# Sliding attention in two pieces instead of three, gate matmuls moved, and the first two row tiles of x transposed on TensorE

## The chip, the core and the metric

The kernel runs on one core of one Trainium2 chip. The metric is the device time of one execution in microseconds (us). A core has five engines that run side by side, each through its own in-order list of instructions: TensorE (PE in the profile; its weight loads are PEld), VectorE (DVE), ScalarE (ACT), GpSimd (POOL) and SyncE (SP), which here only issues DMA transfers.

## The reference

Two attention blocks on the same x (2048 rows, 1024 columns, bf16) are mixed by a gate. Each has 32 heads of width 32.

```python
x = A_x
g = _sigmoid((x * gate_w).sum(-1, keepdims=True))
a = _A_ref(x, A_wqkv, A_wo)      # linear attention
b = _B_ref(x, B_wqkv, B_wo)      # sliding, dilated attention
return g * a + (1 - g) * b

# A: q, k, v = split of x @ wqkv; phi(t) = where(t > 0, t + 1, exp(t)) + 1e-6
#    kv = sum_s phi(k) v;  z = sum_s phi(k);  o = (phi(q) kv) / (phi(q) z + 1e-6);  a = o @ wo
# B: row s sees the W = 8 rows s, s-2, ..., s-14 (dil = 2; rows below 0 are masked)
#    attn = softmax(q k * Dh**-0.5) over them;  o = attn v;  b = o @ wo
```

## The kernel before

**Parity.** A row of B sees only rows of its own parity, so all work is split into two halves p of 1024 rows (even and odd rows). In a half the window is 8 neighbouring rows. A half has 8 row tiles of 128 rows; row tile t of the kernel is tile t % 8 of half t // 8. x is held transposed in `xT[p]`; `xt_load` (L88) brings one row tile by a transposing DMA on SP.

**Products.** Most matrix products are done as seven block products of half-sized blocks in place of eight (a Strassen scheme). A `Group` (L238) is one such product: m1, m2, m3, m6, m4, m7, m5, each four matmuls of 512 columns (named a product here; out groups have eight). Sums of blocks of x (`xsums`, into SS) and of weights (`Weights.sums`, into T, TS) are made on VectorE ahead of use. Two PSUM banks, X and Y, serve a group: m1 writes X, ScalarE copies it to M1s; m6 adds onto X, ScalarE copies it to U2s; m5 adds onto X, copied to U4s; m3 adds onto X and ScalarE writes the result out. m2, m7 and m4 use Y, and VectorE adds M1s, U4s or U2s to it. `run` (L413) interleaves a group g with the one before it, p, in the order m1(g), m2(g), m3(p), m6(g), m4(p), m7(g), m5(g). Groups: vb (V of B), k and q (of B, for 8 heads and one half), ka and va (K and V of A), qa, and out.

**Side work.** After each product `side` lets a step of a queue in: generators yield (delay, length), and a step is taken when its delay is over and the last one's length has passed. In this way the pieces of B's attention (`attn`, L659), of A's key-value sums (`kv`, L543) and of A's outputs (`qa_out`, L580) are put between products. TensorE and SP follow the program's order as written; for the other engines a scheduler orders the instructions when the kernel is built.

**The sliding attention.** For each of 8 (nn, p), 8 heads as two chunks of four (ch): `scores(t)` multiplies blocks of 57 queries with the 64 keys that they can see, four heads side by side (48 matmuls, L672), ScalarE takes the exponential into PT (L678), VectorE multiplies with the mask `maskp` (L680). `pv(t)` multiplies PT with V (48 matmuls, L690) and with ones for the denominators (8 matmuls over 342 columns, L696); ScalarE forms the reciprocal as exp(-ln) in rB (L702, L704), VectorE copies the numerator to nB (L703) and multiplies into oB (L706), which SP stores in OB_d (L707). A piece t covers a third of the rows of both chunks: 18 blocks of 57 are 1026 rows, so that V_d and OB_d have 1026 rows and kT and qT two columns more than needed. One PSUM tile of four banks (tag "s") serves every side piece in turn: scores, pv, kv and qa_out.

**phi.** When a ka group's row is done, `phi` (L518) takes an exponential of 1024 columns on ScalarE (eA) and three VectorE steps.

**Gates.** `gate(t)` (L438) is 8 matmuls of one column on row tile t of xT, into the PSUM tile gps. Tiles 0 to 7 of half 0 are pairs 0 to 3 (tile c and c + 4), those of half 1 pairs 4 to 7. `gates(4)` stands after `vb_group(2)`, `gates(5)` after `vb_group(3)`.

**Start.** `warm_up` (L451) issues matmuls on zeros. `vb_load(k, j)` brings a quarter of one half of V's weights: (0, 0) on ScalarE's queue, all others on SP. `vb_plain(0, 1)` (L484) computes four row tiles with plain products (the tile K, L495), with groups of three warm-ups between; only then do the Groups begin.

**End.** Plain products of A's queries (`qa_plain`, the tile Q), two qa groups, and eight out groups. The oA pieces feed POOL (obA), SP stores them in OA_d, and `out_load` (L757) reads OB_d and, by transposing DMA, OA_d into oT for the out groups.

Of the kernel before, what the change touches and what calls it, by code (L numbers as in the profile page):

```python
# [8 lines left out]
ACT = mybir.ActivationFunctionType  # L9
# [8 lines left out]
TW = 6 * QB  # L18
SPAN = 3 * TW
# [8 lines left out]
def kernel(  # L28
# [30 lines left out]
    V_d = [dram.tile([SPAN, D], BF16, name=f"V_d{p}") for p in range(2)]  # L59
    OB_d = [dram.tile([8, P, SPAN], BF16, name=f"OB_d{p}") for p in range(2)]  # L60
# [115 lines left out]
    bview = B_wqkv.rearrange("(k p) n -> p k n", p=P)  # L176
    gw = consts.tile([P, 8], BF16, name="gw")
    nc.gpsimd.dma_start(out=gw[:], in_=gate_w.rearrange("(k p) -> p k", p=P))

    def vb_load(k, j):  # L180
        (nc.scalar if (k, j) == (0, 0) else nc.sync).dma_start(out=W[:, 2 * k:2 * k + 2, 512 * j:512 * j + 512],
                          in_=bview[:, 2 * k:2 * k + 2, 2 * D + 512 * j:2 * D + 512 * j + 512])
    vb_load(0, 0)
    xt_load(0)
    for k in range(1, 4):
        vb_load(k, 0)
    for t in (4, 1, 5):
        xt_load(t)
# [13 lines left out]
    maskp = consts.tile([P, 2, 6, QB], BF16, name="maskp")  # L202
    nc.gpsimd.memset(maskp[:, :, 0, :], 0.0)
    for w in range(8):
        for base in (7 - w, 71 - w):
            nc.gpsimd.affine_select(out=maskp[:, 0, 0, :], in_=maskp[:, 0, 0, :], compare_op=ALU.not_equal,
                                    fill=1.0, base=base, pattern=[[1, QB]], channel_multiplier=-1)
        nc.gpsimd.affine_select(out=maskp[0:64, 1, 0, :], in_=maskp[0:64, 1, 0, :], compare_op=ALU.not_equal,
                                fill=1.0, base=-w, pattern=[[1, QB]], channel_multiplier=-1)
    nc.gpsimd.tensor_copy(out=maskp[64:P, 1, 0, :], in_=maskp[64:P, 0, 0, :])  # L210
    for e in range(1, 6):
        nc.gpsimd.tensor_copy(out=maskp[:, 0, e, :], in_=maskp[:, 0, 0, :])
        nc.gpsimd.tensor_copy(out=maskp[:, 1, e, :], in_=maskp[:, 1 if e == 3 else 0, 0, :])
    ones = consts.tile([P, 32], BF16, name="ones")
    nc.gpsimd.memset(ones[:], 1.0)
    for p in range(2):
        nc.gpsimd.dma_start(out=V_d[p][1024:SPAN, :].rearrange("r (a e) -> (r a) e", e=P), in_=warm[0:16, 0:P])
# [128 lines left out]
    def step(force=False):  # L346
        seen = set()
        for entry in list(queue):
            if entry[4] in seen:
                continue  # L350
            seen.add(entry[4])
            if not force and (entry[0] > state["now"] or state["free"] > state["now"]):
                continue
            state["free"] = state["now"] + entry[3]
            try:
                delay, entry[3] = next(entry[1])
                entry[0] = state["now"] + delay
                state["steps"] += 1
                return True
            except StopIteration:  # L360
                queue.remove(entry)
                return step(force)
        return False
# [90 lines left out]


# [28 lines left out]
    def vb_plain(*pairs):  # L484


        vs = {pair: v_tiles("va") for pair in pairs}
        tiles = [(pair, i) for pair in pairs for i in range(2)]

        def ps_of(pair, i):  # L490
            return ps_pj.tile([P, 512], F32, name="K", tag="XY"[i] + str(pair % 2))

        def mm(ps, pair, i, j, kc):
            p, c = divmod(pair, 4)
            nc.tensor.matmul(ps[:], lhsT=xT[p][:, kc, i, c * P:c * P + P],  # L495
                             rhs=wvB.W[:, kc, 512 * j:512 * j + 512], start=kc == 0, stop=kc == 7,
                             skip_group_check=True)
        for pair, i in tiles:
            ps = ps_of(pair, i)
            for kc in range(8):  # L500
                if (pair, i) == tiles[0] and kc in (2, 4, 6):
                    warm_up(3)
                mm(ps, pair, i, 0, kc)
            gate(tile_of(pair, i))
            v_final(vs[pair], True)(i, 0, ps[:], None)
        tiles = tiles[2:] + tiles[:2]
        ps = {t: ps_of(*t) for t in tiles}
        for k in range(4):
            for t in tiles:
                for kc in (2 * k, 2 * k + 1):  # L510
                    mm(ps[t], *t, 1, kc)
                if k == 3:
                    pair, i = t
                    v_final(vs[pair], True)(i, 1, ps[t][:], None)
                    vb_store(vs[pair], pair, i)
# [24 lines left out]
    def va_group(w, pair):  # L540
        vs = v_tiles("vA")

        def kv():  # L543
# [18 lines left out]
            if last:  # L562
                nc.vector.tensor_tensor(out=KVz[:].rearrange("p c (g e) -> p c g e", g=4),
                                        in0=KVacc[:, :, None, :].broadcast_to([P, 8, 4, 33]),
                                        in1=bd[:, None, :, :].broadcast_to([P, 8, 4, 33]), op=ALU.mult)
            yield 2, 2
# [89 lines left out]
    def q_of(t, j, b):  # L656
        return TW * t + 2 * QB * j + QB * b

    def attn(nn, p, kT, qT, vw):  # L659

        def scores(t):
            s = side_ps("s")
            for ch in range(2):
                for j in range(3):
                    e = (3 * ch + j) * QB
                    for b in range(2):
                        q0 = q_of(t, j, b)
                        k0 = max(0, q0 - 7)  # L670
                        for g in range(4):
                            nc.tensor.matmul(s[64 * b:64 * b + 64, g, e:e + QB],  # L672
                                             lhsT=kT[32 * g:32 * g + 32, 1024 * ch + k0:1024 * ch + k0 + 64],
                                             rhs=qT[32 * g:32 * g + 32, 1024 * ch + q0:1024 * ch + q0 + QB],
                                             start=True, stop=True)
            PT = ptp.tile([P, 4, TW], BF16, name="PT", tag="PT")
            with tc.high_priority():
                nc.scalar.activation(out=PT[:], in_=s[:, :, 0:TW], func=ACT.Exp, scale=SCALE)  # L678
            m = maskp[:, 0 if t else 1, :, :].rearrange("p i q -> p (i q)")
            nc.vector.tensor_tensor(out=PT[:], in0=PT[:], in1=m[:, None, :].broadcast_to([P, 4, TW]), op=ALU.mult)  # L680
            return PT

        def pv(t, PT):
            o = side_ps("o")
            for e in range(6):
                ch, j = divmod(e, 3)
                for g in range(4):
                    for b in range(2):
                        rows = slice(64 * b, 64 * b + 64)
                        nc.tensor.matmul(o[32 * g:32 * g + 32, 2 * b, QB * e:QB * e + QB],  # L690
                                         lhsT=vw[rows, 3 * t + j, 4 * ch + g, :],
                                         rhs=PT[rows, g, QB * e:QB * e + QB], start=True, stop=True)
            for g in range(4):
                for b in range(2):
                    rows = slice(64 * b, 64 * b + 64)
                    nc.tensor.matmul(o[32 * g:32 * g + 32, 2 * b + 1, 0:TW], lhsT=ones[rows, :], rhs=PT[rows, g, :],  # L696
                                     start=True, stop=True)
            nB = ofp.tile([P, 2, TW], F32, name="nB", tag="nB", bufs=1)
            rB = ofp.tile([P, 2, TW], F32, name="rB", tag="rB", bufs=1)
            oB = ofp.tile([P, 6, 2, QB], BF16, name="oB", tag="oB", bufs=2)  # L700
            with tc.high_priority():
                nc.scalar.activation(out=rB[:], in_=o[:, 1:4:2, 0:TW], func=ACT.Ln)  # L702
                nc.vector.tensor_copy(out=nB[:], in_=o[:, 0:4:2, 0:TW])  # L703
            nc.scalar.activation(out=rB[:], in_=rB[:], func=ACT.Exp, scale=-1.0)  # L704
            num, r = (ap.rearrange("p b (e q) -> p e b q", e=6) for ap in (nB[:], rB[:]))
            nc.vector.tensor_tensor(out=oB[:], in0=num, in1=r, op=ALU.mult)  # L706
            nc.sync.dma_start(out=OB_d[p][2 * nn:2 * nn + 2, :, TW * t:TW * t + TW].rearrange("c p q -> p c q"),  # L707
                              in_=oB[:].rearrange("p (c j) b q -> p c (j b q)", c=2))

        last = None  # L710
        yield 0, 2
        for t in range(4):
            if t < 3:
                PT = scores(t)
                yield (1, 3) if last else (3, 3)
            if last:
                pv(*last)
                yield 1, 3
            last = (t, PT)

    def load_v(nn, p):
        vw = vwp.tile([P, NPAIR, 8, 32], BF16, name="vw", tag="vw")
        for b, j, n in ((0, 0, 1), (0, 1, 8), (1, 0, 9)):
            k0 = max(0, q_of(0, j, b) - 7)
# [7 lines left out]
    def k_group(w, nn, p):  # L732
        kT = kqp.tile([P, 2050], BF16, name="kT", tag="kq")
        nc.gpsimd.memset(kT[:, 2048:2050], 0.0)
        its[nn, p] = kT
        return Group(col_ops(w, p), lambda i, j, ps, add: acc(kT[:, 1024 * j + 512 * i:1024 * j + 512 * i + 512], ps, add))

    def q_group(w, nn, p):
        qT = kqp.tile([P, 2050], BF16, name="qT", tag="kq")
        nc.gpsimd.memset(qT[:, 2048:2050], 0.0)  # L740
# [5 lines left out]
        return Group(col_ops(w, p), lambda i, j, ps, add: acc(qT[:, 1024 * j + 512 * i:1024 * j + 512 * i + 512], ps, add), done)  # L746
# [89 lines left out]
    warm_up(24)  # L836
# [27 lines left out]
    for f in (ws[0], ws[1], xs[0], xs[1], ws[2], xs[3], ws[3], xs[2]):  # L864
        f()
# [4 lines left out]
    gates(4)  # L870
# [4 lines left out]
    gates(5)  # L875
# [104 lines left out]
```

## Time and profile before

| what | value |
|---|---|
| median of 3 runs | 463.4 us (463.18 to 464.05) |
| the profiled execution | 462.85 us, of which 461.1 us are the span |
| TensorE busy | 450.9 us (98%), 5137 matmuls |
| VectorE, ScalarE, GpSimd busy | 286.1, 241.6, 56.6 us |
| moved by DMA | 51.65 MB |

The span runs from the first to the last instruction. In a timeline line stand the start and the length of a run of like instructions, the engine (PE, DVE, ACT), the line of the kernel, operation, written tile <- read tiles, shapes and count; in brackets the idle time before it and what ended it. Lengths of matmuls overlap, since they are pipelined, so what a matmul costs is seen from start to start. In a line of the waits stand who waited for whom, then the total in us, the number of times, and the longest.

### The profile page before, as it was taken

Reading aid. Unit: us, or ns where it says so; the run is one execution under the profiler, and the core shown is the slowest. Engines: PE = TensorE matmul, PEld = TensorE weight load, DVE = VectorE, ACT = ScalarE, POOL = GpSimd, SP = SyncE. Lnnn points to the kernel's source line nnn. Section 1 sums busy time; section 2 is a strip of 40 time slices with the busy share of each in tenths; the row PEclk is TensorE's granted clock in tenths of the full one; section 3 lists DMA queues with packets and bytes.
Section 4 is the critical chain, followed back from the end, with each engine's and each line's share of the span. In section 5 each row is a group of like instructions: output and inputs, shape, how many; then the busy total and the mean of one; then the engine's idle time right before and its main releaser. Section 6 shows DMA issues by size and latency. Waiting matters only on the chain. (4 is left out here: it accounts for less than half of the span.)

```text
span 461.1 us, 11964 instructions
## 1 busy us (share of the span) xinstructions
PE 450.9 (98%) x5137; PEld 217.7 (47%) x5137; DVE 286.1 (62%) x458; ACT 241.6 (52%) x367; POOL 56.6 (12%) x130
## 2 busy tenths in 40 slices
PE   8989999999999999999999999999999999999997
PEld 5445444444444444444444444445554444444444
DVE  0547668769848577486684856579876973164312
ACT  1233447568568386584855848536676545222221
POOL 8000000000000000000000000006676313000000
PEclk9999999999999999999999999999999999999999
DMA  8999811590211702106021066464239872699211
GB/s 180 187 221 246 275 41 64 147 256 19 57 28 33 157 21 64 22 20 159 18 71 28 17 146 181 112 188 103 68 77 205 177 171 81 118 189 174 68 47 46
DMA packets 117941, 51.65 MB, mean 112 GB/s; under 512 B 77696, under 2 KB 115840, under 8 KB 117888
## 3 DMA queue, kind: packets, MB, share of 16 engines
q1 hardware_dynamic: 117520, 50.62, 47.1%
q8 instruction: 40, 0.66, 0.6%
q10 hardware_dynamic: 272, 0.26, 0.2%
q0 software_dynamic: 96, 0.01, 0.1%
q14 instruction: 13, 0.11, 0.1%
HBM read 25.69 MB, written 16.79 MB: 92 GB/s over the span
## 5 line engine op out<-in xcount | busy, mean ns | idle before, releaser
L252 PEld LDWEIGHTS <-xT 128*128 128x128 bf16 (+1 forms) x352 | 32.6, 98 | 37.6 <-issue 0.6
L252 PE MATMUL X<-T,SS 128*128 128x512 f16 x176 | 45.2, 379 | 0.0
L635 PE MATMUL Q<-xT,WS 128*128 128x512 bf16 x192 | 43.9, 379 | 0.5 <-DVE vA L234 0.5
L261 ACT COPY U4s<-X 128x512 f32<-128x512 f32 x40 | 23.2, 581 | 37.3 <-PE X L252 37.2
L252 PEld LDWEIGHTS <-WS 128*128 128x128 bf16 (+1 forms) x288 | 27.1, 98 | 32.9 <-issue 2.5
L678 ACT ACTIVATE PT<-s 128x1368 bf16<-128x1368 f32 x24 | 31.5, 1314 | 19.9 <-PE s L672 19.9
L252 PE MATMUL Y<-W,xT 128*128 128x512 bf16 (+1 forms) x152 | 39.1, 380 | 0.0
L252 PEld LDWEIGHTS <-SS 128*128 128x128 f16 x264 | 24.4, 98 | 27.8
L252 PE MATMUL Y<-xT,WS 128*128 128x512 bf16 (+1 forms) x144 | 37.0, 379 | 0.2 <-DVE qT L234 0.2
L252 PE MATMUL X<-SS,TS 128*128 128x512 f16 x144 | 36.9, 379 | 0.1
L680 DVE TENSOR_TENSOR PT<-PT,maskp 128x1368 bf16<-128x1368 bf16 x24 | 20.8, 867 | 20.8 <-ACT PT L678 20.8
L252 PEld LDWEIGHTS <-TS 128*128 128x128 f16 x216 | 20.5, 98 | 25.2 <-issue 1.8
L261 ACT COPY M1s<-X 128x512 f32<-128x512 f32 x40 | 23.3, 583 | 11.8 <-PE X L252 11.7
L261 ACT COPY U2s<-X 128x512 f32<-128x512 f32 x40 | 23.3, 582 | 10.4 <-PE X L252 10.4
L635 PEld LDWEIGHTS <-WS 128*128 128x128 bf16 x192 | 18.2, 98 | 20.6 <-issue 0.8
L252 PEld LDWEIGHTS <-oT 128*128 128x128 bf16 (+1 forms) x176 | 17.1, 98 | 21.8 <-DMA oT<-OA_d 1.5
L703 DVE COPY nB<-o 128x684 f32<-128x684 f32 x24 | 20.8, 867 | 6.3 <-ACT rB L702 6.0
L603 POOL TENSOR_TENSOR obA<-ofv,rec 128x512 bf16<-128x512 f32 x22 | 24.0, 1109 | 0.9
L640 ACT ACTIVATE eq<-Q 128x512 bf16<-128x512 f32 x24 | 14.3, 598 | 18.4 <-PE Q L635 17.3
L252 PE MATMUL X<-T,oS 128*128 128x512 f16 x96 | 22.7, 379 | 0.0
L252 PE MATMUL X<-W,SS 128*128 128x512 bf16 x88 | 22.7, 380 | 0.0
L252 PE MATMUL X<-W,xT 128*128 128x512 bf16 x88 | 22.6, 380 | 0.0
(137 smaller groups left out, 759.6 us busy)
## 6 DMA issues: line engine op xcount, KB each, us to landing
OB_d<-oB SPq DMA_DIRECT2D x24, 171.0 KB, 2.9
V_d<-va SPq DMA_DIRECT2D x16, 256.0 KB, 3.0
WS<-in_B_wqkv_dram SPq DMA_DIRECT2D x16, 256.0 KB, 4.2
W<-in_A_wqkv_dram SPq DMA_DIRECT2D x8, 512.0 KB, 7.0
OA_d<-obA SPq DMA_DIRECT2D x16, 256.0 KB, 2.4
out_dram<-osb SPq DMA_DIRECT2D x30, 128.0 KB, 2.0
oT<-OB_d SPq DMA_DIRECT2D x12, 256.0 KB, 4.8
vw<-V_d SPq DMA_DIRECT2D x8, 288.0 KB, 4.7
```

The source lines that it names most:

```text
L252: nc.tensor.matmul(ps[:], lhsT=lhsT, rhs=rhs, start=start and kc == 0, stop=kc == self.nk - 1, skip_group_check=True)
L261: nc.scalar.copy(out=s[:], in_=ps[:])
L603: nc.gpsimd.tensor_tensor(out=ob[:, k:k + 2], in0=of[:, k:k + 2, :, 0:32], in1=rec[:, k:k + 2].broadcast_to([P, 2, 8, 32]), op=ALU.mult)
L635: nc.tensor.matmul(ps[:], lhsT=w.W[:, kc, j * P:j * P + P], rhs=xT[p][:, kc, i, :], start=kc == 0, stop=kc == 7, skip_group_check=True)
L640: nc.scalar.activation(out=es[i][:, j, :], in_=ps[:], func=ACT.Exp)
L678: nc.scalar.activation(out=PT[:], in_=s[:, :, 0:TW], func=ACT.Exp, scale=SCALE)
L680: nc.vector.tensor_tensor(out=PT[:], in0=PT[:], in1=m[:, None, :].broadcast_to([P, 4, TW]), op=ALU.mult)
L703: nc.vector.tensor_copy(out=nB[:], in_=o[:, 0:4:2, 0:TW])
```

## The change

- **Pieces**: `scores` and `pv` take one chunk of four heads over all 1024 rows (9 pairs of blocks, the last of 56 instead of 57): 72 matmuls a piece in place of 48, the exponential and the mask over 4 x 512 columns, the ones over 512. There are two pieces of each kind instead of three. Their order is scores, scores, pv, pv instead of scores, scores, pv, scores, pv, pv, with other delays between. oB has one buffer instead of two. One mask serves all pieces, and V_d, OB_d, kT and qT have exactly 1024 rows or columns; the fills for the rows beyond are gone. `load_v` issues four DMAs instead of three.
- **Gates**: `gates(4)` moves behind `vb_group(3)`.
- **Start**: row tiles 0 and 4 are loaded as they are (`xr`), and TensorE transposes them (8 transposes each, with an identity made on POOL) into PSUM, from where ScalarE and VectorE copy one half each into xT. 14 warm-ups stand ahead instead of 24, and none between. The first sums on VectorE are issued after the last of these copies.
- **Guard**: oA pieces are not taken before KVz is computed.

```diff
+    ident = consts.tile([P, P], BF16, name="ident")
+    nc.gpsimd.memset(ident[:], 0.0)
+    nc.gpsimd.affine_select(out=ident[:], in_=ident[:], compare_op=ALU.not_equal, fill=1.0, base=0,
+                            pattern=[[1, P]], channel_multiplier=-1)
...
-    vb_load(0, 0)
-    xt_load(0)
-    for k in range(1, 4):
-        vb_load(k, 0)
-    for t in (4, 1, 5):
+    xr = {}
+
+    def xr_load(t):
+        xr[t] = ering.tile([P, D], BF16, name="xr", tag="e")
+        nc.sync.dma_start(out=xr[t][:], in_=xrows(t))
+    vb_load(0, 0, nc.scalar)
+    xr_load(0)
+    vb_load(1, 0)
+    vb_load(2, 0)
+    vb_load(3, 0)
+    xr_load(4)
+    for t in (1, 5):
         xt_load(t)
...
-    maskp = consts.tile([P, 2, 6, QB], BF16, name="maskp")
-    nc.gpsimd.memset(maskp[:, :, 0, :], 0.0)
+    maskp = consts.tile([P, 512], BF16, name="maskp")
+    nc.gpsimd.memset(maskp[:], 0.0)
...
     for w in range(8):
...
+        diagonal(slice(0, QB), -w)
+        diagonal(slice(QB, 2 * QB), 7 - w)
+        diagonal(slice(QB, 2 * QB), 71 - w)
+        diagonal(slice(8 * QB, 512), 72 - w)
...
-    for p in range(2):
-        nc.gpsimd.dma_start(out=V_d[p][1024:SPAN, :].rearrange("r (a e) -> (r a) e", e=P), in_=warm[0:16, 0:P])
...
+            if entry[4] == "oa" and "KVz" not in ready:
+                continue
...
+    def transpose(t):
+        p, j = divmod(t, 8)
+        hf, c = divmod(j, 4)
+        for k0, tag, copy in ((0, "X1", nc.scalar.copy), (4, "Y1", nc.vector.tensor_copy)):
+            tps = ps_pj.tile([P, 512], F32, name="tps", tag=tag)
+            tps = tps.bitcast(BF16)[:, 0:512].rearrange("p (k n) -> p k n", k=4)
+            for k in range(4):
+                nc.tensor.transpose(tps[:, k, :], xr[t][:, (k0 + k) * P:(k0 + k + 1) * P], ident[:])
+            with tc.high_priority():
+                last_dve[0] = copy(out=xT[p][:, k0:k0 + 4, hf, c * P:(c + 1) * P], in_=tps).ins
...
             for kc in range(8):
-                if (pair, i) == tiles[0] and kc in (2, 4, 6):
-                    warm_up(3)
+                if (pair, i) == tiles[0] and kc in (0, 6):
+                    transpose(tile_of(pair, kc // 6))
                 mm(ps, pair, i, 0, kc)
...
+    def block(j, b):
+
+        q0 = 2 * QB * j + (QB if j < 8 else QB - 1) * b
+        return q0, QB if j < 8 else QB - 1, min(max(0, q0 - 7), 960)
...
+        def scores(ch):
             s = side_ps("s")
...
+            for j in range(NPAIR):
+                for b in range(2):
+                    q0, n, k0 = block(j, b)
+                    for g in range(4):
+                        nc.tensor.matmul(s[64 * b:64 * b + 64, g, QB * j:QB * j + n],
+                                         lhsT=kT[32 * g:32 * g + 32, ch, k0:k0 + 64],
+                                         rhs=qT[32 * g:32 * g + 32, ch, q0:q0 + n], start=True, stop=True)
+            PT = ptp.tile([P, 4, 512], BF16, name="PT", tag="PT")
             with tc.high_priority():
-                nc.scalar.activation(out=PT[:], in_=s[:, :, 0:TW], func=ACT.Exp, scale=SCALE)
...
+                nc.scalar.activation(out=PT[:], in_=s[:], func=ACT.Exp, scale=SCALE)
+            nc.vector.tensor_tensor(out=PT[:], in0=PT[:], in1=maskp[:, None, :].broadcast_to([P, 4, 512]), op=ALU.mult)
             return PT
...
+                    nc.tensor.matmul(o[32 * g:32 * g + 32, 2 * b + 1, :], lhsT=ones[rows, :], rhs=PT[rows, g, :],
                                      start=True, stop=True)
...
+            oB = ofp.tile([P, 1024], BF16, name="oB", tag="oB", bufs=1)
             with tc.high_priority():
...
+                nc.scalar.activation(out=rB[:], in_=o[:, 1:4:2, :], func=ACT.Ln)
+                nc.vector.tensor_copy(out=nB[:], in_=o[:, 0:4:2, :])
             nc.scalar.activation(out=rB[:], in_=rB[:], func=ACT.Exp, scale=-1.0)
...
+            nc.sync.dma_start(out=OB_d[p][2 * nn + ch, :, :], in_=oB[:])
...
-        last = None
-        yield 0, 2
-        for t in range(4):
-            if t < 3:
-                PT = scores(t)
-                yield (1, 3) if last else (3, 3)
-            if last:
-                pv(*last)
-                yield 1, 3
-            last = (t, PT)
+        yield 0, 4
+        PT = [scores(0)]
+        yield 1, 4
+        PT.append(scores(1))
+        for ch in range(2):
+            yield 1, 3
+            pv(ch, PT[ch])
+        yield 1, 3
...
-        for b, j, n in ((0, 0, 1), (0, 1, 8), (1, 0, 9)):
+        for b, j, n in ((0, 0, 1), (0, 1, 8), (1, 0, 8), (1, 8, 1)):
...
-        kT = kqp.tile([P, 2050], BF16, name="kT", tag="kq")
-        nc.gpsimd.memset(kT[:, 2048:2050], 0.0)
+        kT = kqp.tile([P, 2, 1024], BF16, name="kT", tag="kq")
...
-    warm_up(24)
+    warm_up(14)
...
+    with tc.issue_after(last_dve[0]):
+        for f in (ws[0], ws[1], xs[0], xs[1], ws[2], xs[3], ws[3], xs[2]):
+            f()
     later(2, lambda: gates(3))
...
     run(lambda: vb_group(2), 0)
     x_loads(6, 7)
-    gates(4)
     defer(1, xsums(4) + xsums(1))
     run(lambda: vb_group(3), 0)
...
-    gates(5)
+    gates(4, 5)
```

## The prediction

> **What bounds the kernel now.** I read the page's first part, the waits of TensorE, and then the timeline of each stage that the change touches.
>
> ```profile
> span 461.1 us, 11964 instructions
> ...
> PE 450.9 (98%) x5137; PEld 217.7 (47%) x5137; DVE 286.1 (62%) x458; ACT 241.6 (52%) x367; POOL 56.6 (12%) x130
> ```
> ```profile
> PE gps L442 <- DMA xT<-in_A_x_dram: 1.5, 2, 1.1
> ...
> PE X L252 <- DMA oT<-OA_d: 1.0, 1, 1.0
> ...
> PE s L672 <- DVE nB L703: 0.6, 1, 0.6
> PE Q L635 <- DVE vA L234: 0.5, 1, 0.5
> ```
>
> TensorE is busy 98% of the span, so time moves only by work that leaves TensorE's in-order stream, or by waits that leave it or enter it. The start (TensorE timeline):
>
> ```profile
> 1.20 4.52 PE L453 MATMUL gps<-KVacc 128*128 128x256 bf16 x24 [1.20 <-DVE KVacc L171]
> 5.56 0.59 PE L495 MATMUL K<-W,xT 128*128 128x512 bf16 x2
> ...
> 7.39 0.59 PE L495 MATMUL K<-W,xT 128*128 128x512 bf16 x2 [0.91 <-DMA W<-in_B_wqkv_dram]
> ...
> 9.04 0.59 PE L495 MATMUL K<-W,xT 128*128 128x512 bf16 x2
> ```
>
> The first tile of K moves at the pace of W: its last three blocks land at 7.35, 8.03 and 9.00 us. From 9.04 the stream is dense. Then the gates:
>
> ```profile
> 27.00 1.03 PE L252 MATMUL X<-T,SS 128*128 128x512 f16 x4
> 28.45 0.35 PE L442 MATMUL gps<-gw,xT 128*128 128x1 bf16 x8 [0.43 <-DMA xT<-in_A_x_dram]
> 29.91 0.35 PE L442 MATMUL gps<-gw,xT 128*128 128x1 bf16 x8 [1.11 <-DMA xT<-in_A_x_dram]
> 30.12 1.02 PE L252 MATMUL X<-W,xT 128*128 128x512 bf16 x4
> ```
>
> TensorE stands before row tiles that have not landed. Last, one attention on TensorE, and ScalarE beside it:
>
> ```profile
> 134.60 0.57 PE L672 MATMUL s<-qT,kT 32*64 32x57 bf16 x48
> 135.11 1.04 PE L252 MATMUL X<-W,SS 128*128 128x512 bf16 x4
> ...
> 138.16 0.37 PE L696 MATMUL o<-PT,ones 64*32 64x342 bf16 x8
> 138.46 1.04 PE L252 MATMUL Y<-xT,WS 128*128 128x512 f16 x4
> ...
> 140.20 1.03 PE L252 MATMUL X<-W,xT 128*128 128x512 bf16 x4
> 141.27 0.56 PE L672 MATMUL s<-qT,kT 32*64 32x57 bf16 x48
> ```
> ```profile
> 135.24 1.31 ACT L678 ACTIVATE PT<-s 128x1368 bf16<-128x1368 f32 x1 [0.81 <-PE s L672]
> 136.45 0.58 ACT L232 CAST tA<-X 128x512 bf16<-128x512 f32 x1
> 137.06 1.06 ACT L520 ACTIVATE eA<-tA 128x1024 bf16<-128x1024 bf16 x1
> 138.03 0.57 ACT L261 COPY U2s<-X 128x512 f32<-128x512 f32 x1
> ```
>
> A product (4 matmuls) takes 0.864 us from start to start. m5 starts two products after m6's end and adds onto the bank that U2s copies; m3, two products after m5's, onto the one that U4s copies. A copy that is late stops TensorE. The ScalarE queue is in order.
>
> **The change part by part** (profiled execution: 462.85 us with a span of 461.1; median of the runs 463.4, so 0.55 more).
>
> *Pieces.* From start to start, a scores piece of 48 matmuls adds 0.595 us to TensorE, a PV piece of 48+8 0.755. In the single records 32 matmuls go at once (0.14 us), then after a break of 0.10 one each 8.35 ns; a piece also pays about 0.09 to enter and, in scores, 0.13 to leave. With 72 matmuls: scores 0.595 + 24 x 0.00835 = 0.795. PV: 0.755 + 0.200 + the longer tail of the ones, 170 columns more at 0.42 ns = 0.071 (all eight run side by side, or the tail would be longer than 0.25): 1.026. Each of 8 attentions: before 3 x (0.595 + 0.755) = 4.05, after 2 x (0.795 + 1.026) = 3.64. Saved 0.41 x 8 = 3.3 us.
>
> *Waits that go with the old order.* Scores 3 waits for nB at 3 products after PV 1: 0.12 us in six attentions (141.27 above: due at 141.16), 0.63 in the first; and the 0.5 before Q at 302 (0.65 from start to start), behind the last PV piece, which now lies four products ahead. Gone: 0.7 + 0.6 + 0.65 = 2.0.
>
> *The new wait.* The pieces are now scores, 4 products, scores, 4, PV, 3, PV. The second scores comes right after m3 of a ka group, and ScalarE's order becomes: tA cast, first phi exponential (eA), PT, U2s; before, PT went ahead of both. Counted from m3's start in the seven attentions that have a ka group: cast at 0.864 + 0.20 = 1.06; eA 0.61 later, 1.67; ScalarE is free 0.96 on, 2.63. The scores are over by 0.864 + 0.795 = 1.66, so PT waits for eA. PT's length: 1.314 us for 1368 columns, 0.735 for 684, hence 0.84 ns a column and 1.88 for 2048; the next starts 0.1 before its end, so U2s runs 4.41 to 4.99. m5 is due at 1.66 + 2.59 = 4.25 and starts at 5.05: **0.80 us of wait, 7 times, 5.6 us.** Behind it on TensorE everything stands; on ScalarE the second eA and U4s go later, which the PV piece doesn't need. In the scores before (after m7) U4s ends at 2.49 with m3 due at 2.59: hidden, by 0.05 to 0.1 only.
> PV 2 needs nB: Ln over 1024 is 1.02 (0.735 + 340 x 0.84 ns), nB after it 1.22 (0.867 for 684 columns, 0.686 for 512, so 1.05 ns a column), and 2.6 are there; the mask over 2048 (1.2), kT and eA stand ahead of nB on VectorE, which makes it about even (0.05 each), and 0.65 late in the second attention, where two of wvA's 1.22 us sums lie between. Cost 0.95. With one oB, the second oB waits on VectorE for the OB_d store (2.9 us to land): about 1 us, with va's add queued behind it; that add has a product to spare, so nothing.
>
> *Gates.* From 27.86, where the last product ends, to 30.12 are 2.26 us, of which 16 gate matmuls take 0.40 where nothing is late. Moved one group (6 us) later they meet landed tiles (the next pair lands at 31.1 and 32.7): saved 1.86. Their number stays. Group 3 itself needs only pair 3, whose gates ran without a wait at 24.87, and its last VectorE sum is at 29.7, with its m7 due at 32.2.
>
> *Start.* Removed: 10 warm-ups ahead and 9 between. Added: 16 transposes, four copies, and the identity on POOL (its gw issue, 1.08 us, lies between; ready near 3). On SP a plain load issues in 0.46 us against 1.3, and lands in 0.8 us steps (W: 14.18, 14.97, 15.68) against 1.4 for transposing ones. So vb1 to vb3 land near 5, 6 and 6.5, xr 4 near 7.3. TensorE: 14 warm-ups at 0.213 end at 4.2; 8 transposes and a copy (0.58 plus 0.2 of delay) put the first K at 5.4; two thirds of a tile, then the wait for xr 4; transposes, rest, gates: the second tile at about 8.8 against 9.84. Gain 1.0, between -0.3 and 1.7. Behind the new copies stand, on ScalarE, the va casts (the first is due only after a whole tile), and on VectorE wvB's sums, which wait for W's second half anyway (15.06 before, near 12 now). In VectorE's new order the sum of row tile 6 stands ahead of the second W sum; even if that tile lands at 19.95 as before, this W sum is over at 21.5 and the x sum after it at 21.9, with m6 due at 24.3. The other four sums need 3.1 us more, to 25.0, with m7 due at 25.1: just hidden, and with earlier x tiles by 2 us.
> The transposes' price: the nearest row is the gate, 8 loads of 128x128 weights with a short matmul in 0.20 to 0.37 us; a warm-up of 256 columns takes 0.109. I take 0.06 to 0.11 each. The Trainium skill (TensorE: Matmul & The Clock Gate, Part 4: PE-mode transpose) speaks against it: about 275 ns each in a kernel, and transposes do not count as busy for the clock. At 275 ns, 16 take 4.4 us and the start loses about 0.8. The row decides: a warm-up too lasts 0.42 us by its record, at 0.21 from start to start. On the clock the trace says that warm-ups run 0.213 apart up to 4.6 us and 0.109 from 4.9; the same page (Part 1) asks for about 3.4 us of activity. Fourteen last only 3.0. If the half clock stays until 8, six K matmuls take 0.43 instead of 0.216, partly under the wait for W: the gain falls to 0.2.
>
> *The rest.* Fewer waits for credits put the eighth oA piece four Q matmuls (0.86 us) earlier against out(0), whose wait for oT hangs on it over POOL, the OA_d store and SP (13.3 us from piece to landing, TensorE's work 12.5): saved 0.86. Nothing: 8 more vw issues against 8 fewer OB_d on SP, hidden since SP waits 161 us for oB; two V_d fills and 16 small memsets off POOL, and a mask of 32 selects instead of 24, done near 12 us and first used at 103; the oa guard. Without that cover the mask would cost 0.18 us a select.
>
> Sum: -3.3 - 2.0 + 5.6 + 0.95 - 1.86 - 1.0 - 0.86 = -2.5, thus 460.4 in the profiled execution and **460.9 us** as a median.
>
> **Rivals.**
> *The ScalarE stall is not there* (0.10): if eA comes after PT on the chip as before, 5.6 and the nB cost go: 455. For it: ScalarE is idle 48%. Against: its program order is fixed.
> *The start gives nothing* (0.14): cold clock, or xr 4 after 8 us: 462 to 462.6. For it: fourteen warm-ups are short. Against: transposes and K follow at once.
> *PT costs more than its columns* (0.18, slower): four full banks in one exponential. Each 0.1 us on top adds 0.7 to the seven waits, and past the 0.05 of slack it also delays U4s and so m3, in all eight attentions, and in the first attention's m5. The sign turns at 2.07 instead of 1.88 us (7 x 0.19 + 9 x 0.14 = 2.5); at 2.15 it is 7 x 0.27 + 9 x 0.22 = 3.9 us: 464.8. For it: slack of 0.05 is all there is. Against: 684 and 1368 columns, and 1056 in a copy at 1.036, lie on one line.
>
> **How the numbers follow.** The forecast has 0.58, 459.3 to 462.3. What a measurement can tell is 0.2%, 0.9 us: faster is below 462.5. Faster: 0.56 of the forecast, 0.10, and 0.04 of the start rival: 0.70; the same: 0.02 + 0.10: 0.12; slower 0.18. The range leaves out the first rival and half of the last: 458.6 to 463.8.
>
> **What would show it.** Right: PT 128x2048 at 1.88 us with eA just before it in seven attentions, TensorE waiting for ACT U2s about 0.8 each; no gps wait near 28; scores at 0.8 and PV at 1.03 from start to start; K's second tile near 8.8. Wrong: no such wait for U2s, a wait of m3 for U4s, or K matmuls 0.43 apart.

## The result, and the profile after

| | before | after |
|---|---|---|
| median | 463.29 us (4 runs, 462.98 to 464.05) | 460.69 us (4 runs, 460.46 to 461.02) |
| ratio of the times | | 0.9942, interval 0.9925 to 0.9959 |
| the profiled execution | 462.85 us | 460.67 us |

The changed kernel is 2.6 us faster by the medians, 2.2 by the two profiled executions. In the experiments below, ten of the 25 executions of the kernel before have a mean granted clock of 0.995 or 0.996 and a median 1.7 us above that of the other 15, which have 0.999 or 1.0; "at full clock" means there an execution at 0.998 or more. The first part of its page, and all waits of TensorE:

```profile
span 458.9 us, 11765 instructions
...
PE 446.0 (97%) x5070; PEld 216.0 (47%) x5070; DVE 282.9 (62%) x452; ACT 237.1 (52%) x345; POOL 60.8 (13%) x119
```
```profile
PE X L264 <- ACT U2s L273: 4.5, 7, 0.7
PE tps L476 <- DMA xr<-in_A_x_dram: 1.2, 1, 1.2
PE gps L467 <- DVE KVacc L170: 1.2, 1, 1.2
PE K L520 <- DMA W<-in_B_wqkv_dram: 0.7, 1, 0.7
PE o L712 <- DVE nB L724: 0.6, 1, 0.6
PE K L520 <- ACT xT L478: 0.5, 1, 0.5
PE o L712 <- issue: 0.3, 1, 0.3
```

Of the four waits that were shown of before (gates for xT, X for oT, scores for nB, Q for vA) none is left. In their place stand seven waits for U2s, one PV that waits for nB, and, at the start, one for the second row tile of x. These rows count idle time between the modelled ends of matmuls; from start to start the seven U2s waits are 0.77, 0.77, 0.83, 0.83, 0.83, 0.83 and 0.83 us, together 5.69, against 4.5 in the row.

One attention on TensorE, and ScalarE beside it, at the same place as before (the m5 that waits starts at 137.21):

```profile
133.14 0.77 PE L696 MATMUL s<-qT,kT 32*64 32x57 bf16 x72
133.84 1.04 PE L264 MATMUL X<-SS,TS 128*128 128x512 f16 x4
...
135.57 1.03 PE L264 MATMUL Y<-xT,WS 128*128 128x512 f16 x4
137.21 1.02 PE L264 MATMUL X<-SS,TS 128*128 128x512 f16 x4 [0.61 <-ACT U2s L273]
138.16 0.74 PE L712 MATMUL o<-PT,vw 64*32 64x57 bf16 x72
```
```profile
133.24 0.59 ACT L244 CAST tA<-X 128x512 bf16<-128x512 f32 x1 [0.68 <-PE X L264]
133.86 1.06 ACT L545 ACTIVATE eA<-tA 128x1024 bf16<-128x1024 bf16 x1
134.82 1.86 ACT L701 ACTIVATE PT<-s 128x2048 bf16<-128x2048 f32 x1
136.58 0.58 ACT L273 COPY U2s<-X 128x512 f32<-128x512 f32 x1
```

ScalarE runs these four back to back: cast, eA, PT, U2s. The scores end near 133.9, yet PT starts only when eA is done, and U2s, which m5 needs, ends at 137.16, just ahead of m5's start at 137.21.

The gates have lost their wait; the product at 27.91 follows the one at 27.05 at 0.86, and all 32 gate matmuls run together later:

```profile
27.05 1.03 PE L264 MATMUL X<-T,SS 128*128 128x512 f16 x4
27.91 1.03 PE L264 MATMUL X<-W,xT 128*128 128x512 bf16 x4
...
33.96 0.94 PE L456 MATMUL gps<-gw,xT 128*128 128x1 bf16 x32
34.76 1.02 PE L264 MATMUL X<-W,xT 128*128 128x512 bf16 x4
```

The start, in the timeline of TensorE, with the one long piece of the chain of waits in that stretch below it:

```profile
1.20 3.05 PE L467 MATMUL gps<-KVacc 128*128 128x256 bf16 x14 [1.20 <-DVE KVacc L170]
4.16 0.62 PE L476 MATMUL tps<-ident,xr 128*128 128x128 bf16 x8
5.23 1.04 PE L520 MATMUL K<-W,xT 128*128 128x512 bf16 x4 [0.45 <-ACT xT L478]
6.99 0.59 PE L520 MATMUL K<-W,xT 128*128 128x512 bf16 x2 [0.72 <-DMA W<-in_B_wqkv_dram]
8.82 0.62 PE L476 MATMUL tps<-ident,xr 128*128 128x128 bf16 x8 [1.24 <-DMA xr<-in_A_x_dram]
...
9.91 1.89 PE L520 MATMUL K<-W,xT 128*128 128x512 bf16 x8
```
```profile
2.67 6.10 DMA xr<-in_A_x_dram
```

The second tile of K starts at 9.91, against 9.84 before. Its row tile was issued at 2.67 and landed at 8.77; before, it was issued at 3.78 and landed at 9.80.

The balance of the two traces, term by term, from start to start on TensorE:

| term | predicted | measured |
|---|---|---|
| pieces: 24 x (0.594 + 0.755) against 16 x (0.792 + 1.025) | -3.3 | -3.3 |
| old waits for nB (0.7 in six, 0.6 in one) and of Q (0.65) | -2.0 | -1.95 |
| the new wait for U2s | +5.6 | +5.7 |
| PV waits for nB (0.65 in the second attention, 0.11 in the last, 0.04 in three) | +0.95 | +0.86 |
| gates | -1.86 | -1.87 |
| start | -1.0 | +0.07 |
| out's wait for oT | -0.86 | -1.16 |
| not in the prediction: waits of 0.23 and 0.38 near 121 and 123 us (the second attention; the page names Y for qT), and oA pieces (0.35) | 0 | -0.95 |
| not in the prediction: a stall inside the last PV piece | 0 | +0.43 |
| sum | -2.5 | -2.2 |

The spans differ by 461.1 - 458.9 = 2.2. The last run of matmuls starts 2.4 us earlier (453.31 against 455.71), and what follows it takes 0.2 longer; so 0.2 us on TensorE lies outside the terms. Most of it is the 0.01 us that a product right behind a piece takes longer, of which there are 16 fewer.

### The profile page after: what moved, and what is told of

Read it like the earlier page. It is cut to its first block, busy times and chain, and to the rows that moved or that the text cites. A ratio compares the mean times of both kernels' runs of the same rounds, so it can differ in the third digit from the quotient of the medians.

```text
span 458.9 us, 11765 instructions
## 1 busy us (share of the span) xinstructions
PE 446.0 (97%) x5070; PEld 216.0 (47%) x5070; DVE 282.9 (62%) x452; ACT 237.1 (52%) x345; POOL 60.8 (13%) x119
## 4 chain that ended last, share of the span: by engine, by line
PE 90%; ACT 6%; DMA 1%; DVE 0%; SPq 0%; issue 0%; ACTq 0%; DVEq 0%
PE X L264 42%; PE Y L264 28%; PE Q L661 9%; PE K L520 3%; ACT PT L701 3%; PE o L712 2%; PE oA L618 2%; ACT eA L545 2%; PE s L696 1%; DMA xr<-in_A_x_dram 1%; PE kps L579 1%; ACT tA L244 1%; PE o L717 1%; PE Y L299 1%; ACT U2s L273 1%; PE gps L456 1%
## 5 line engine op out<-in xcount | busy, mean ns | idle before, releaser
L264 PEld LDWEIGHTS <-WS 128*128 128x128 bf16 (+1 forms) x288 | 28.1, 98 | 33.6
L486 POOL MEMSET vA<- 128x32 bf16 x16 | 4.0, 250 | 268.3 <-DVE eA L548 144.9
L701 ACT ACTIVATE PT<-s 128x2048 bf16<-128x2048 f32 x16 | 29.9, 1869 | 15.1 <-PE s L696 15.0
L702 DVE TENSOR_TENSOR PT<-PT,maskp 128x2048 bf16<-128x2048 bf16 x16 | 19.6, 1224 | 22.1 <-ACT PT L701 22.1
L629 POOL TENSOR_TENSOR obA<-ofv,rec 128x512 bf16<-128x512 f32 x22 | 25.7, 1187 | 0.9
L724 DVE COPY nB<-o 128x1024 f32<-128x1024 f32 x16 | 19.5, 1220 | 6.0 <-ACT rB L723 6.0
L723 ACT ACTIVATE rB<-o 128x1024 f32<-128x1024 f32 x16 | 16.4, 1025 | 12.3 <-DVE oB L730 9.5
```

Of the source, the lines that this page charges most:

```text
L264: nc.tensor.matmul(ps[:], lhsT=lhsT, rhs=rhs, start=start and kc == 0, stop=kc == self.nk - 1, skip_group_check=True)
L629: nc.gpsimd.tensor_tensor(out=ob[:, k:k + 2], in0=of[:, k:k + 2, :, 0:32], in1=rec[:, k:k + 2].broadcast_to([P, 2, 8, 32]), op=ALU.mult)
L701: nc.scalar.activation(out=PT[:], in_=s[:], func=ACT.Exp, scale=SCALE)
L702: nc.vector.tensor_tensor(out=PT[:], in0=PT[:], in1=maskp[:, None, :].broadcast_to([P, 4, 512]), op=ALU.mult)
L723: nc.scalar.activation(out=rB[:], in_=o[:, 1:4:2, :], func=ACT.Ln)
L724: nc.vector.tensor_copy(out=nB[:], in_=o[:, 0:4:2, :])
```

## The experiments

Four kernels ran beside 25 executions of the kernel before, with a median of 464.38 us (462.95 to 466.17). Those at full clock have a median of 463.58, and differences in us below are against that.

**The pieces alone.** The changed kernel with the old start (the first sums on VectorE are not held back either) and the old place of the gates:

```diff
...
-    xr_load(0)
-    vb_load(1, 0)
-    vb_load(2, 0)
-    vb_load(3, 0)
-    xr_load(4)
-    for t in (1, 5):
+    xt_load(0)
+    for k in range(1, 4):
+        vb_load(k, 0)
+    for t in (4, 1, 5):
         xt_load(t)
...
-                if (pair, i) == tiles[0] and kc in (0, 6):
-                    transpose(tile_of(pair, kc // 6))
+                if (pair, i) == tiles[0] and kc in (2, 4, 6):
+                    warm_up(3)
...
-    warm_up(14)
+    warm_up(24)
...
+    gates(4)
     defer(1, xsums(4) + xsums(1))
...
-    gates(4, 5)
+    gates(5)
```

> The kernel before with the two-piece attention alone: old start, gates(4) where it was. Forecast's terms: pieces -3.3, old waits -2.0, oT -0.86, U2s waits +5.6, nB waits +0.95: +0.4 by the forecast; with the waits as the changed kernel's trace has them (oT's 1.15 and the 0.6 near 121 gone too, 1.3 of nB and PV waits) about 0.2 to 0.7 below before. Rival (the pieces are the whole gain and gates and start give nothing): -2.6.

Measured: 463.11 us (462.61 to 464.72), ratio 0.998, interval 0.9964 to 0.9995. The 11 of its 12 executions at full clock have a median of 463.05, 0.5 less than before. From the waits of TensorE:

```profile
PE X L257 <- ACT U2s L266: 4.5, 7, 0.7
PE gps L449 <- DMA xT<-in_A_x_dram: 1.5, 2, 0.9
...
PE o L705 <- issue: 0.6, 1, 0.6
PE o L705 <- DVE nB L717: 0.6, 1, 0.6
PE X L257 <- DMA oT<-OA_d: 0.3, 1, 0.3
```

The seven U2s waits, the nB wait and the shrunken oT wait come with the pieces, and so does the stall ("issue") in the last PV; the gates' wait stays. The prediction's own terms for this part, -3.3 - 2.0 + 5.6 + 0.95 - 0.86, give +0.4; by the medians it came out 0.9 lower, about the size of the unforeseen 0.95. The two profiled executions don't show that difference: here the span is 461.4 us, 0.3 above before. The packing as such is worth nearly nothing here: what it takes off TensorE goes into the wait for ScalarE.

**The gates alone.** The kernel before, with one line moved:

```diff
-    gates(4)
     defer(1, xsums(4) + xsums(1))
     run(lambda: vb_group(3), 0)
...
-    gates(5)
+    gates(4, 5)
```

> The kernel before with gates(4) moved behind vb_group(3), nothing else. Forecast: -1.9, because the two waits near 28 us go and the gates meet landed tiles. Rival: the wait goes to the first product of vb_group(4) or comes back before oT, then 0 to -1.

Measured: 461.72 us (461.21 to 462.33), ratio 0.9943, interval 0.9924 to 0.9962; 1.9 us less than before. Its waits hold no gps for xT, and the wait for oT has not shrunk (1.0 in the row before):

```profile
PE X L252 <- DMA oT<-OA_d: 1.2, 1, 1.2
```

In the timeline, from the gates of pair 3 to the next gates are 25.60 to 34.63, 9.03 us, where before they were 11.29 (24.87 to 36.16) with 0.40 of gate matmuls between them that now lie behind: 1.86 saved. The span of this profiled execution, 460.2 us, is only 0.9 below before: in it TensorE comes to the gates of pair 3 later by 0.73 (25.60 against 24.87), though the start is the same. One moved line carries most of what the time shows of the whole change.

**The old start in the changed kernel.** The changed kernel with the loads and warm-ups of the first experiment, and the first sums on VectorE not held back; the gates stay where the change puts them.

> The changed kernel with the start of before: 24 warm-ups and 3 x 3 between, row tiles 0 and 4 by transposing DMA, no transposes on TensorE. If the start gives the 1.0 us that was forecast: 461.7. If, as the trace reads (second K tile at 9.91 us against 9.84), it gives nothing: 460.6 to 460.7, within 0.2 of the changed kernel.

Measured: 461.09 us (460.63 to 461.5), ratio 0.9932, interval 0.9909 to 0.9954, which overlaps the changed kernel's, and 2.5 us less than before, where the changed kernel has 2.6; the span of its profiled execution is 458.9 us, that of the changed kernel. Its timeline of TensorE:

```profile
8.66 0.59 PE L513 MATMUL K<-W,xT 128*128 128x512 bf16 x2
9.09 0.34 PE L449 MATMUL gps<-gw,xT 128*128 128x1 bf16 x8
9.68 1.67 PE L513 MATMUL K<-W,xT 128*128 128x512 bf16 x7 [0.25 <-DMA xT<-in_A_x_dram]
```

Here the second tile of K starts one matmul of 0.216 us ahead of 9.68, at 9.46 (the first of its eight is missing in the records), so with transposing loads and 33 warm-ups it is no later than with the new start, 9.91. Read in the same way, the four traces with the old start give 9.84 (before), 9.84, 10.09 and 9.46, the two with the new one 9.91 and 9.82. One start differs from the next by up to 0.6 us, but the 8.8 of the forecast is in none, and the gain of 1.0 is not there.

**phi later.** The changed kernel, with a ka group's phi put off, so that eA no longer stands ahead of PT:

```diff
+    last_save = [None]
...
-                nc.scalar.copy(out=s[:], in_=ps[:])
+                last_save[0] = nc.scalar.copy(out=s[:], in_=ps[:]).ins
...
-            defer(0, phi(e[:], ts[i][:]))
+            def go():
+                with tc.issue_after(last_save[0]):
+                    defer(0, phi(e[:], ts[i][:]))
+            later(9, go)
```

> The changed kernel with phi's exponentials (eA) of both rows issued 9 products later, behind the copies of the attention's stretch; nothing else. If eA ahead of PT is what makes TensorE wait for U2s: the seven waits of 0.77 to 0.83 go down to under 0.1 each, and the time falls by 5.3 to 5.9 us, to about 455. If PT itself (1.87 us) is too long for the copy behind it: the waits stay at over 0.4 each and the time falls by less than 3.

Measured: 461.33 us (460.24 to 463.85), ratio 0.9947, interval 0.9926 to 0.9968; the four of its 12 executions at full clock have a median of 460.69. Its profiled execution holds 3.4 us at half clock (its mean is 0.996), and has a span of 461.2 us. The longest waits of TensorE, and ScalarE in the attention that was shown above:

```profile
PE o L716 <- issue: 2.4, 1, 2.4
PE o L716 <- DVE nB L728: 1.9, 1, 1.9
PE X L265 <- ACT U4s L274: 1.6, 6, 0.5
```
```profile
134.57 0.59 ACT L245 CAST tA<-X 128x512 bf16<-128x512 f32 x1 [0.68 <-PE X L265]
135.31 1.88 ACT L705 ACTIVATE PT<-s 128x2048 bf16<-128x2048 f32 x1
137.08 0.58 ACT L274 COPY U2s<-X 128x512 f32<-128x512 f32 x1
```

All seven waits for U2s are gone, with PT as long as before: what made them was eA ahead of PT, not PT's length alone. But most of the 5.7 us came back elsewhere. The second attention's PV 2 now waits 1.97 for nB, which on VectorE stands behind a sum of weights and the steps that slipped:

```profile
110.44 1.22 DVE L134 TENSOR_TENSOR T<-W,T 128x2048 f16<-128x2048 bf16 x1
111.57 0.41 DVE L133 TENSOR_TENSOR WS<-WS 128x512 f16<-128x512 bf16 x1
111.91 1.22 DVE L728 COPY nB<-o 128x1024 f32<-128x1024 f32 x1
```

(1.3 more than in the changed kernel). The late eA now stand ahead of U4s copies, for which six products wait 2.5 us in all from start to start, and three more products are 0.5 late. Net, the last attention's PV 2 starts at 287.31 against 288.95 in the changed kernel, 1.64 earlier. Then 3.6 us go at one spot:

```profile
287.31 0.68 PE L716 MATMUL o<-PT,vw 64*32 64x57 bf16 x64
290.43 0.25 PE L716 MATMUL o<-PT,vw 64*32 64x56 bf16 x8 [2.44 <-issue]
290.46 0.65 PE L721 MATMUL o<-PT,ones 64*32 64x512 bf16 x8
291.04 1.89 PE L265 MATMUL X<-T,SS 128*128 128x512 f16 x4
```

The stall of 2.4 us is followed by matmuls of 512 columns 0.43 apart instead of 0.216 (four of X take from 291.04 to 292.71): the granted clock is 0.5 from 290.23 to 293.64. So this kernel shows the cause of the U2s waits, and the version itself wins nothing that can be told from the changed kernel.

## Why the prediction was right or wrong

It said 460.9 and 460.69 came, through a sum with one wrong term and two that were missing. That the sum came so close is in part luck: the start gave 1.07 less than said and an unforeseen stall took 0.43, while waits that the forecast passed over or took as smaller gave 0.95 and 0.3.

- **Pieces.** Right. Scores 0.792 (0.795 said), PV 1.025 (1.026 said): the rate of 8.35 ns for each further matmul, read from single records of the shorter pieces, carried over to 72, and the ones over 512 columns ran side by side as assumed.
- **The new wait.** Right in place and size: 0.77 to 0.83 in the seven attentions with a ka group (0.80 said), PT at 1.87 us (1.88 said). That eA's place in ScalarE's program order is the cause is shown by the experiment that moved it. The rival of no stall (455) falls with these rows, and that of a PT dearer than its columns (464.8) with PT's mean of 1869 ns.
- **PV 2 and nB.** Right in the second attention (0.65, as said). Of the 0.05 in each of the others, 0.04 came in three, 0.11 in the last.
- **Gates.** Right, 1.87, and shown alone by the one-line experiment.
- **The wait for oT.** Said to shrink by 0.86, it left altogether (1.16 from start to start), and in the rows of the three experiments with the new pieces it is down to 0.3, 0.2 and none, while with the gates alone it stayed at 1.2: it goes with the pieces, as argued.
- **The start.** Wrong, 1.0 us. The step that failed is "vb1 to vb3 land near 5, 6 and 6.5, xr 4 near 7.3". They landed at 5.59, 6.95, 8.11 and 8.77. xr 0, vb0 and vb1 landed at 4.11, 4.84 and 5.59, at the pace that was assumed (0.8 us or less for each 256 KB), but from a later first landing. Then the pace broke: vb2 and vb3 took 1.36 and 1.16. The busy share of the DMA engines in tenths, and what they moved, in slices of 0.25 us from 0 to 10 us of the changed kernel:

```profile
DMA  0000000929697999999999699999999983999999
GB/s 0 0 0 0 0 0 0 131 66 279 164 213 279 373 373 385 365 381 381 393 289 148 156 173 188 144 291 356 348 319 300 228 76 44 202 283 282 292 291 288
```

From 5.25 to 6.5 the engines move 144 to 188 GB/s, less than half of what they moved just before, while they are busy nearly throughout. In all six traces such a stretch overlaps with the 32 packets of gw (the 2 KB of gate weights on GpSimd's queue): they run from 5.04 to 6.57 here, and from 3.98 to 5.47 in the kernel before, where the rate falls to 37 to 166 GB/s from 4 to 5.5 us. Whether these packets slow the others is not shown: no kernel without them was run.

The cheaper issue did bring earlier landings: before, the same three blocks of W landed at 7.35, 8.03 and 9.00, and tile 4 at 9.80, 1.03 later than xr 4. What used this up is the order on TensorE. The old start has the last K matmuls and gates of the first tile behind it when tile 4 lands, and the second tile starts 0.04 after the landing (so W was not the only thing that paced the old start: there is a wait of 0.17 for tile 4 as well). In the new start eight transposes (0.46), two K matmuls (0.43) and eight gate matmuls (0.20) come after the landing and ahead of the second tile, 1.1 us together, though the last block of W had landed at 8.11. The rival "the start gives nothing" named a late xr 4 as one of its two ways ("xr 4 after 8 us"), and that one came true. It said 462 to 462.6 for it; the unforeseen gains made up the difference. The other way, a cold clock, is excluded by the traces: full clock from 4.0 us on, and in the experiment with phi later, where it came only at 6.9, the second tile of K started no later (9.82).
- **The transposes' price.** Eight took 0.46 us from 8.82 to 9.28, 0.06 each, though the record of one lasts 0.22. The row of the gates and warm-ups was the right guide; the 275 ns that the Trainium skill gives (TensorE: Matmul & The Clock Gate, Part 4: PE-mode transpose) do not describe transposes in a row here.
- **Missing.** Two short waits near 121 to 123 us and the oA waits (0.95 together) ended with the old order of the pieces. The waits of before listed them ("PE Y L252 <- DVE qT", "PE oA L592 <- ACT ofv"), and the sum passed over them. The stall in the last PV could not be read from before.

Left open in part: the stall inside the last attention's PV 2 (0.3 in its row in the changed kernel, 0.6, 0.5 and 2.4 in the three experiments with the new pieces, none in before and with the gates alone). No engine, tile or transfer of data is named as what ended it. The weight loads of TensorE show where it stands, in the changed kernel and then with the pieces alone:

```profile
288.84 0.68 PEld L712 LDWEIGHTS <-vw 64*32 64x32 bf16 x65 [0.42 <-issue]
289.95 0.11 PEld L712 LDWEIGHTS <-vw 64*32 64x32 bf16 x7 [0.43 <-issue]
```
```profile
290.60 0.65 PEld L705 LDWEIGHTS <-vw 64*32 64x32 bf16 x62 [0.42 <-issue]
291.96 0.12 PEld L705 LDWEIGHTS <-vw 64*32 64x32 bf16 x10 [0.71 <-issue]
```

It comes behind the 65th weight load of the piece in the two kernels with the new start, and behind the 62nd in the two with the old start, which has three matmuls more at its beginning (33 warm-ups against 14 and 16 transposes). So it stands at a fixed number of TensorE instructions from the start of the program, and not at a fixed place of the work. And in each of the four traces a single DMA packet of 16 KB of the kind "instruction" (queue q8) moves shortly before; TensorE goes on 1.36, 1.31, 1.25 and 1.32 us after its end (288.59, 290.65, 288.38 and 289.11). Most likely, then, TensorE waits there for its own next instructions; the traces point to this and name nothing else, but no run moved either side of it. Why the packet comes late there is not shown.

Not tried either was a phi put off by one step only, behind U2s but ahead of U4s. In the trace above ScalarE is idle for 1.17 us between U2s and U4s, and one eA takes 1.06, so by these durations the U2s waits would end and U4s would still be in time; whether the second eA would be is not worked out.

## What to carry to other kernels

Before a transfer is made cheaper, list what stands between its landing and its consumer in the consumer's in-order program, and read what the DMA engines move in that very stretch, not in a later one: here tile 4 landed 1.0 us earlier, and 1.1 us of transposes, K matmuls and gates then stood behind the landing. When pieces of side work are packed, list what stands on every other engine's in-order program between the piece and the next copy that the main stream waits for; here one exponential that came to stand ahead of another set 5.7 us of waits against 3.3 us of saved matmuls. And test moved lines one at a time: the smallest edit of this change, a gate put behind one more group, gave 1.9 of its 2.6 us.

## What the runs showed of the hardware

- **The clock changes in steps of one window.** The stretches at full clock last 457.386 us (before and the pieces alone), 453.973 (after, old start, gates alone), and, with the half clock between them, 283.306 and 167.253 (phi later); the half clock lasts 3.413. These are 134, 133, 83, 49 and 1 times 3.4133 us, to within 0.005 us. One such window at half clock costs a busy TensorE half of it, about 1.7 us by estimate. In the one trace that shows it, it began 0.2 us before the end of the stall of 2.4 us, so that TensorE stood still for 2.2 us of the window before it, and not for all of it. The Trainium skill (TensorE: Matmul & The Clock Gate, Part 1) states such a window, free-running and 3413 ns long; these traces agree to the nanosecond.
- **So the number of warm-ups doesn't fix when the clock comes.** With 24 warm-ups from 1.20 us on, full clock came at 4.78, 5.65, 6.54 and 4.78 us in four kernels; with 14 at 4.00 and 6.92.
- **TensorE seems to wait for its own instructions.** In the kernel before, queue q8 moved 40 packets of kind "instruction", 0.66 MB, beside 5137 matmuls and as many weight loads, some 257 of these to a packet (an estimate). Inside a PV piece of 72 matmuls (0.56 us elsewhere), TensorE stood for 0.3 to 2.4 us (the rows) at the same instruction number in four kernels, until 1.25 to 1.36 us after the end of such a packet.
- **DMA engines can be busy and move little.** In the changed kernel they moved 352 GB/s from 3 to 4 us and 218 from 5.5 to 7, at busy shares of 0.99 and 0.97; in the kernel before 91 GB/s from 4 to 5.5, at 0.82.
